# Partial sums of an MLP added to blocks in DRAM by GpSimd's adding DMAs instead of by VectorE in SBUF

## The chip, the core and the metric

The kernel runs on one core of a Trainium2 chip. Its time is the device time of one execution, in microseconds (us). The core has five queues of instructions that run side by side and wait for each other by semaphores: TensorE (PE in the profile; its weight loads are PEld), VectorE (DVE), ScalarE (ACT), GpSimd (POOL) and SyncE (SP), which here only issues DMAs. SBUF is the memory on the chip, PSUM the one that TensorE writes to, DRAM the memory beside it. Each engine takes its instructions strictly in the order in which they stand in its queue, so an instruction that waits holds up all behind it.

## The reference

```python
xn = layernorm(x)                                    # x: 2048 x 576, float32
a  = xn @ dft_hid_re.T ;  b = xn @ dft_hid_im.T      # 576 x 576 each
y  = dft_seq_re @ a - dft_seq_im @ b                 # 2048 x 2048 each
m  = relu(xn @ w1) @ w2                              # w1: 576 x 4608, w2: 4608 x 576
out = x + y + m
```

The result is the sum of x, a two-dimensional Fourier transform (its real part) and an MLP, all of the same normalized x.

## The kernel before

All products are made with fp16 operands split into a high and a low part, three matmuls for one product, summed in float32 in PSUM.

**Stages.** First x is loaded, normalized, split and transposed, in 16 tiles of 128 rows, four of which make a group (`NG` = 4 groups of 512 rows); the first steps of the MLP are woven in between, and the last four tiles (12 to 15) are normalized while the first products of the second layer run. Then comes the MLP (`NB` = 9 blocks of 512 hidden columns, each for the 4 groups: 36 steps), then the transform along the hidden dimension (`dft1`), then the one along the sequence.

**A step of the MLP** computes the hidden columns of one block for one group (`mlp1_step`, L291 and L316, then relu and split in `mlp1_out`, L331 to L342), while the second layer (`mlp2`, L356) of the step before runs between: four parts of `mlp1` and, after them, products 0 and 1, 2 and 3, 4 and 5, and 6. These seven products are those of a fast (Strassen-like) scheme: the group's 512 x 576 result is cut into four blocks (row, column), and `PRODUCTS` says which block each product adds to. In the list below the last two figures are that block's row and column; where the third entry is `False`, the product accumulates onto an earlier one in PSUM (`PLACE`), whose running sum is then added to another block, too.

```python
PRODUCTS = [(A11, B11, True, 0, 0), (A12, B21, True, 0, 0), (S2, T2, False, 0, 1),
            (S1, T1, True, 1, 1), (S3, T3, False, 1, 1), (S4, B22, False, 0, 1), (A22, T4, False, 1, 0)]
PLACE = [0, 1, 0, 3, 0, 3, 0]
```

After each product VectorE adds the PSUM sum, times a scale `us[b]`, to a block of the float32 accumulator `accs[g]` in SBUF (L362). The accumulator starts as x itself, since x is loaded into it (`load_x`), and the normalization reads it there. There are two PSUM buffers for products (`ps2`); the transposes of x use the same two. A product that goes into a buffer, or accumulates onto it, waits until its last sum has been read.

When the last block's product 6 of a group is added, the group's four tiles are stored to DRAM (`spill`, L365), and the memory of `accs` is given to the transforms, whose first results `R` lie there. In the last stage `load_out` loads the stored sums again, and L851 adds the transform to them.

**Beside this**, `prepare_block` readies the weights of the next block in small steps: maxima (L98, then over partitions by GpSimd, L104), scales (L107 to L112, L422 to L432), splits (L165 on ScalarE, L166 on VectorE), sums of w2's blocks (L438 to L441). `passes` loads the matrices of the sequence transform once to sum their magnitudes on ScalarE (L663). The order of instructions on each engine is worked out by a scheduler when the program is built; `tc.issue_after(order["acc"])` puts an instruction of VectorE behind the newest addition to the accumulator.

Of the kernel before, what the change touches and what calls it, by code (L numbers as in the profile page):

```python
# [1 line left out]

# [7 lines left out]
F32 = mybir.dt.float32  # L10
BF16 = mybir.dt.bfloat16
I32 = mybir.dt.int32
AF = mybir.ActivationFunctionType
ALU = mybir.AluOpType
# [3 lines left out]
P = 128  # L18
S = 2048
D = 576  # L20
DFF = 4608
NT = S // P
FB = 512
NB = DFF // FB
# [3 lines left out]
NG = S // G  # L28
TG = G // P
# [4 lines left out]
EH = D // 2  # L34
# [7 lines left out]
def kernel(  # L42
# [17 lines left out]
    nc = tc.nc  # L60
# [3 lines left out]
    dram = ctx.enter_context(tc.tile_pool(name="dram", bufs=1, space=bass.MemoryType.DRAM))  # L64
# [8 lines left out]

    accs = [accp.tile([P, TG, D], F32, name=f"acc{g}") for g in range(NG)]
    acc = [accs[t // TG][:, t % TG] for t in range(NT)]
    spill = [dram.tile([P, D], F32, name=f"spill{t}") for t in range(NT)]
    raws = {}

    def load_x(t):
# [16 lines left out]
    def magnitude(dst, src):  # L96

        nc.vector.tensor_reduce(dst, src, AX.XY, ALU.max, apply_absolute_value=True)  # L98

    def power(s, p, m):  # L100

        n = m.shape[-1]
        top = small.tile([P, 16], F32, tag="top", name="top")[:, :n]
        nc.gpsimd.partition_all_reduce(top, m, P, ReduceOp.max)  # L104
        yield
        half = small.tile([P, 16], F32, tag="half", name="half")[:, :n]
        nc.vector.tensor_scalar(half, top, 2.0**-100, 0.5, ALU.max, ALU.mult)  # L107
        nc.vector.tensor_scalar(  # L108
            s.bitcast(I32), half.bitcast(I32), EXPONENT, EXPONENT,
            ALU.bitwise_and, ALU.bitwise_xor,  # L110
        )
        nc.vector.tensor_scalar(  # L112
            p.bitcast(I32), half.bitcast(I32), EXPONENT, None, ALU.bitwise_and
        )
# [45 lines left out]
    def cell(tag, n=NQ):  # L160
        return small.tile([P, n], F32, tag=f"c_{tag}", name=f"c_{tag}", bufs=2)
# [9 lines left out]
    means, factors, shifts, order = {}, {}, {}, {}  # L171
# [115 lines left out]
    w1s, w2s, us, hs = {}, {}, {}, {}  # L287

    def mlp1_group(b, g, i, cols, ps, wk=WK, start=True, stop=True):
        for n, (kx, hl, k) in enumerate(wk):  # L290
            nc.tensor.matmul(  # L291
                ps[:, cols], w1s[b, i // 2][:, hl, i % 2 * KT + k], xT[g][:, kx, cols],
                start=(start and n == 0), stop=(stop and n == len(wk) - 1),
            )

    def new_ps1(b, g, i):
        return ps1.tile([P, G], F32, tag="ps1", name=f"p1_{b}_{g}_{i}")

    def mlp1(b, g, i):
        ps = new_ps1(b, g, i)  # L300
        mlp1_group(b, g, i, slice(0, G), ps)
        return ps
# [39 lines left out]
        order["lo"] = nc.vector.tensor_tensor(lo, st[:, 1:], hi, ALU.subtract).ins  # L342

    places = {}

    def mlp2(b, g, n):

        qa, qb, first, row, col = PRODUCTS[n]
        if first:
            places[n] = ps2.tile([P, 2, 512], F32, tag="ps2", name=f"p2_{b}_{g}_{n}")[:, :, :EH]  # L350
        ps = places[PLACE[n]]
        for c in range(2):
            for i in range(NQ):
                h, w = hs[b, g, i], w2s[b, i]
                for j, (x, y) in enumerate(((0, 0), (0, 1), (1, 0))):
                    nc.tensor.matmul(  # L356
                        ps[:, c], h[:, x, qa, c * P : (c + 1) * P], w[:, y, qb],
                        start=first and i == 0 and j == 0, stop=i == NQ - 1 and j == 2,
                        skip_group_check=not first,
                    )  # L360
        o = accs[g].rearrange("p (h c) (j e) -> p h j c e", h=2, j=2)[:, row, col]
        order["acc"] = nc.vector.scalar_tensor_tensor(o, ps, us[b], o, ALU.mult, ALU.add).ins  # L362
        if b == NB - 1 and n == 6:
            for t in range(g * TG, (g + 1) * TG):
                nc.sync.dma_start(spill[t], acc[t])  # L365

    sc, pw, mx = {}, {}, {}

    def max_w1(b, f):

        i, r = divmod(f, 2)
        if f == 0:
            mx["w1", b], sc["w1", b], pw["w1", b] = cell("mw1"), cell("sw1"), cell("pw1")
        if r == 0:
            mx["f", b] = cell("mf", 2)
            mx["b", i] = small.tile([P, 1], BF16, tag=f"mb{i}", name=f"mb{b}_{i}") if b < 2 else None
        with tc.issue_after(order["acc" if b > 1 else "lo"]) if b else nullcontext():
            magnitude(mx["f", b][:, r : r + 1], raws["w1", b, i][:, r * KT : (r + 1) * KT])
        if r:
            m = mx["w1", b][:, i : i + 1] if b > 1 else mx["b", i]  # L380
            nc.vector.tensor_reduce(m, mx["f", b], AX.X, ALU.max)

    def later(step):

        with tc.issue_after(order["acc"]):
            next(step, None)

    def power_w1(b, i):
# [62 lines left out]
    def prepare_w1(b, i):  # L451
        p = power_w1(b, i)
        return [
            lambda: max_w1(b, 2 * i),
            lambda: (max_w1(b, 2 * i + 1), b > 1 and next(p)),
            lambda: later(p),
        ], [
            lambda: split_w1(b, 2 * i),
            lambda: split_w1(b, 2 * i + 1),
        ]  # L460
# [40 lines left out]
    ps = [ps1.tile([P, G], F32, tag="ps1", name=f"p1_0_0_{i}") for i in range(NF)]  # L501
# [15 lines left out]
    fill(64)  # L517

    weave(stats([0]), no, no, no, lambda: max_w1(0, 0))
    N(0)  # L520
    max_w1(0, 1)
# [66 lines left out]
    T(10)  # L588
    T(11)
    early = [mlp1(0, 2, 0), mlp1(0, 2, 1)]  # L590
    for q in range(7):
        mlp2(0, 0, q)

# [15 lines left out]
    def power_d(j):  # L609
        if j == 0:  # L610
            sc["d"], pw["d"], mx["d"] = cell("sd", 4), cell("pd", 4), cell("md", 4)
        m = slice(j, j + 1)
        with tc.issue_after(order["acc"]):
            magnitude(mx["d"][:, m], raws["d", j])
        yield from power(sc["d"][:, m], pw["d"][:, m], mx["d"][:, m])

# [24 lines left out]
    NP = NT // 2  # L641
# [28 lines left out]
    for n in range(2, len(steps)):  # L670
        b, g = steps[n]
        pb, pg = steps[n - 1]
        if g == 0 and b:
            if b + 1 < NB:
                todo += prepare_block(b + 1)
            else:
                todo += [lambda: (load_d(0), load_d(1)), lambda: None, new_d, lambda: None]
                for j in range(4):
                    d = power_d(j)
                    todo += [lambda d=d: next(d), lambda d=d, j=j: (later(d), split_d(j))]  # L680
                    if j < 2:
                        todo += [lambda j=j: load_d(j + 2), lambda: None]
                todo += [scales_d]
# [3 lines left out]
        ps = []  # L687
        for i in range(NF):
# [6 lines left out]
            if b == 0 and g + 1 < NG:  # L695
                t = (g + 1) * TG + i
# [15 lines left out]
    for q in range(7):  # L712
        mlp2(*steps[-1], q)
# [109 lines left out]
    def load_out(p):  # L823
        o = outs[p] = op.tile([P, 2, D], F32, tag="o", name=f"o{p}")
        for h in range(2):
            nc.sync.dma_start(o[:, h], spill[p + h * NP])

    AHEAD = 3
    load_out(0)
    for n, (p, kh) in enumerate(units):  # L830
        if kh == 0 and p + 1 < NP:
            load_out(p + 1)
        if n + 1 < len(units):
            load_c(n + 1)
        for i, (q, rq, first, row, col) in enumerate(PRODUCTS):
            m = n * 7 + i
            if m + AHEAD < 7 * len(units):
                operand(m + AHEAD)
            if first:
                places[i] = bank(f"p{n}_{i}")  # L840
            ps, w = places[PLACE[i]], csp[m]
            for k in range(HK):
                r = R[kh * HK + k]
                for j, (a, c) in enumerate(((0, 0), (0, 1), (1, 0))):
                    nc.tensor.matmul(  # L845
                        ps, w[:, a, k], r[:, c, rq],
                        start=first and k == 0 and j == 0, stop=k == HK - 1 and j == 2,
                        skip_group_check=not first,
                    )
            o = outs[p][:, row, col * EH : (col + 1) * EH]  # L850
            nc.vector.scalar_tensor_tensor(o, ps, us["c"][:, n : n + 1], o, ALU.mult, ALU.add)  # L851
            if kh and i in (2, 4, 5, 6):
                h, j = ((0, 0), (1, 1), (0, 1), (1, 0))[(2, 4, 5, 6).index(i)]
                rows = slice((p + h * NP) * P, (p + h * NP + 1) * P)
                e = slice(j * EH, (j + 1) * EH)
                nc.sync.dma_start(out[rows, e], outs[p][:, h, e])
# [54 lines left out]
```

## Time and profile before

| | us |
|---|---|
| median of 3 runs | 1286.96 (1286.81 to 1287.19) |
| profiled execution, its own time | 1287.1 |
| its span in the trace | 1285.3 |
| first addition to the accumulator (L362) | starts at 68.91 |
| one step of the MLP, in the steady part | 22.16 |
| last matmuls of `mlp2`, first stores of the last group | about 842 |

The span runs from the first to the last instruction of the trace; 1.8 us of the execution's time lie around it. In the lines of the profile, a group of instructions reads: line, engine, operation, what is written <- what is read, shape, count | busy us in total, mean ns of one | idle time of the engine ahead of them, and who ended it. In a timeline the first two figures are the start and the length in us.

### The profile page before, as it was taken

What the parts mean: (1) busy time and instruction counts of PE and PEld (TensorE: products, weight loads), DVE (VectorE), ACT (ScalarE), POOL (GpSimd) and SP (SyncE); (2) the same over time, 40 slices, a digit from 0 to 9 for tenths busy, and PEclk for the clock granted to TensorE, in tenths of its full rate; (3) what the DMA queues carried; (4) which work ended last, traced back from release to release, by engine and by line L of the source; (5) the groups of instructions that cost most, each with busy time, mean ns of one, the idle gap of its engine ahead of it and who ended that gap; (6) DMA issues with size and microseconds to landing.
All of it is one profiled execution on the core that took longest, in us unless ns stands there. A gap on an engine that the chain in (4) does not pass through costs nothing.

```text
span 1285.3 us, 21854 instructions
## 1 busy us (share of the span) xinstructions
PE 1267.4 (99%) x9164; PEld 862.8 (67%) x9164; DVE 982.2 (76%) x1671; ACT 539.0 (42%) x794; POOL 34.1 (3%) x60
## 2 busy tenths in 40 slices
PE   8799999999999999999999999999999999999998
PEld 7565666666565665666565665677777777777777
DVE  8978877786686687777867878567678787888875
ACT  4834343443443443534434434234443334333332
POOL 2210000000000000000000000000000000000000
PEclk9999999999999999999999999999999999999999
DMA  6002112221222222222222313330023435344320
GB/s 242 35 8 61 56 65 91 86 73 69 87 91 67 65 79 68 68 91 87 70 70 87 96 58 109 122 120 18 1 106 126 157 101 168 112 133 132 130 85 19
DMA packets 38002, 112.75 MB, mean 88 GB/s; under 512 B 3984, under 2 KB 10640, under 8 KB 37904
## 3 DMA queue, kind: packets, MB, share of 16 engines
q1 hardware_dynamic: 37904, 111.36, 25.9%
q8 instruction: 71, 1.16, 0.4%
q14 instruction: 27, 0.22, 0.1%
HBM read 101.91 MB, written 9.44 MB: 87 GB/s over the span
## 4 chain that ended last, share of the span: by engine, by line
PE 91%; DVE 4%; DMA 2%; ACT 2%; issue 1%; SPq 0%; POOLq 0%; ACTq 0%; DVEq 0%
PE p L291 29%; PE p L356 27%; PE p L845 26%; PE pd L743 7%; PE p L316 1%; DMA raw_w<-in_w_dram 1%; DVE acc L362 1%; DMA acc<-in_x_dram 0%; ACT xT L248 0%; DMA f<-in_cre_dram 0%; DMA c<-in_cre_dram 0%; DVE xn L225 0%; DVE w1s L166 0%; DVE w2s L166 0%; ACT xn L226 0%
## 5 line engine op out<-in xcount | busy, mean ns | idle before, releaser
L291 PE MATMUL p<-xT,w1s 128*128 128x512 f16 (+1 forms) x2136 | 435.4, 355 | 1.5 <-ACT xT L248 1.1
L356 PE MATMUL p<-w2s,h 128*128 128x288 f16 x3024 | 394.4, 286 | 0.4 <-DVE h L342 0.2
L356 PEld LDWEIGHTS <-h 128*128 128x128 f16 x3024 | 295.3, 98 | 101.1 <-issue 0.9
L845 PE MATMUL p<-R,cs 128*128 128x288 f16 x2688 | 329.4, 286 | 0.0
L291 PEld LDWEIGHTS <-w1s 128*128 128x128 f16 x2136 | 192.7, 98 | 201.3 <-issue 18.0
L845 PEld LDWEIGHTS <-cs 128*128 128x128 f16 x2688 | 263.0, 98 | 66.3
L362 DVE SCALAR_TENSOR_TENSOR acc<-p,c_ub,acc 128x576 f32<-128x576 f32 x252 | 204.6, 813 | 38.4 <-PE p L356 38.0
L165 ACT ACTIVATE cs<-c,sc_c 128x1024 f16<-128x1024 f32 x112 | 128.5, 1149 | 200.5 <-PE p L845 147.3
L166 DVE SCALAR_TENSOR_TENSOR cs<-c,sc_c,cs 128x1024 f16<-128x1024 f32 x112 | 143.6, 1283 | 50.3 <-ACT cs L165 50.2
L335 DVE SCALAR_TENSOR_TENSOR h<-p,h 128x256 f16<-128x256 f32 (+1 forms) x144 | 79.7, 555 | 94.3 <-ACT h L334 94.1
L341 ACT ACTIVATE h<-s 128x1024 f16<-128x1024 f32 x72 | 76.1, 1057 | 161.3 <-DVE s L339 161.3
L334 ACT ACTIVATE h<-p 128x512 f16<-128x512 f32 (+1 forms) x144 | 69.8, 486 | 143.9 <-PE p L291 141.6
L342 DVE TENSOR_TENSOR h<-s,h 128x1024 f16<-128x1024 f32 x72 | 88.1, 1224 | 31.4 <-ACT h L341 30.4
L743 PE MATMUL pd<-dsp,xT 128*128 128x288 f16 x896 | 110.4, 286 | 0.1
L743 PEld LDWEIGHTS <-xT 128*128 128x128 f16 x896 | 87.7, 98 | 22.5 <-issue 0.5
L851 DVE SCALAR_TENSOR_TENSOR o<-p,us_c,o 128x288 f32<-128x288 f32 x112 | 57.5, 513 | 20.0 <-PE p L845 19.9
L663 ACT ACTIVATE f<-f 128x1024 f32<-128x1024 f32 x64 | 66.7, 1041 | 3.7 <-DMA f<-in_cre_dram 3.7
L331 ACT ACTIVATE s<-p 128x256 f32<-128x256 f32 x72 | 27.5, 381 | 71.8 <-PE p L316 54.4
L165 ACT ACTIVATE w2s<-raw_w,c_sw 128x576 f16<-128x576 f32 (+1 forms) x54 | 43.9, 850 | 26.1 <-DVE raw_w L439 15.6
L166 DVE SCALAR_TENSOR_TENSOR w2s<-raw_w,c_sw,w2s 128x576 f16<-128x576 f32 (+1 forms) x54 | 48.3, 914 | 7.6 <-ACT w2s L165 7.6
L166 DVE SCALAR_TENSOR_TENSOR w1s<-raw_w,c_sw,w1s 128x640 f16<-128x640 f32 x36 | 30.8, 894 | 9.9 <-ACT w1s L165 9.9
L165 ACT ACTIVATE w1s<-raw_w,c_sw 128x640 f16<-128x640 f32 x36 | 27.9, 819 | 23.8 <-DVE c_sw L108 23.6
(102 smaller groups left out, 663.2 us busy)
## 6 DMA issues: line engine op xcount, KB each, us to landing
f<-in_cre_dram SPq DMA_DIRECT2D x32, 512.0 KB, 3.5
f<-in_cim_dram SPq DMA_DIRECT2D x32, 512.0 KB, 3.5
c<-in_cre_dram SPq DMA_DIRECT2D x32, 512.0 KB, 4.3
c<-in_cim_dram SPq DMA_DIRECT2D x32, 512.0 KB, 4.5
raw_w<-in_w_dram SPq DMA_DIRECT2D x17, 640.0 KB, 4.0
raw_w<-in_w_dram SPq DMA_DIRECT2D x18, 576.0 KB, 3.7
acc<-in_x_dram SPq DMA_DIRECT2D x16, 288.0 KB, 6.0
spill<-acc SPq DMA_DIRECT2D x16, 288.0 KB, 2.5
```

Of the source, the lines that this page charges most:

```text
L165: nc.scalar.activation(hi, src, AF.Copy, scale=s)
L166: nc.vector.scalar_tensor_tensor(lo, src, s, hi, ALU.mult, ALU.subtract)
L291: nc.tensor.matmul(ps[:, cols], w1s[b, i // 2][:, hl, i % 2 * KT + k], xT[g][:, kx, cols], start=(start and n == 0), stop=(stop and n == l ...
L334: nc.scalar.activation(hi, src, AF.Relu)
L335: stt(lo, src, 0.0, hi, ALU.max, ALU.subtract)
L341: order["s"] = nc.scalar.activation(hi, st[:, 1:], AF.Copy).ins
L342: order["lo"] = nc.vector.tensor_tensor(lo, st[:, 1:], hi, ALU.subtract).ins
L356: nc.tensor.matmul(ps[:, c], h[:, x, qa, c * P : (c + 1) * P], w[:, y, qb], start=first and i == 0 and j == 0, stop=i == NQ - 1 and j == 2 ...
L362: order["acc"] = nc.vector.scalar_tensor_tensor(o, ps, us[b], o, ALU.mult, ALU.add).ins
L663: nc.scalar.activation(f, f, AF.Abs, scale=2.0**-10, accum_out=sums_c[:, n, q : q + 1])
L743: nc.tensor.matmul(ps[j], xT[g][:, kx, c * P : (c + 1) * P], dsp[j][:, hl, k], start=(n == 0), stop=(n == len(XK) - 1),)
L845: nc.tensor.matmul(ps, w[:, a, k], r[:, c, rq], start=first and k == 0 and j == 0, stop=k == HK - 1 and j == 2, skip_group_check=not first,)
```

## The change

The sum of a product is no longer added by VectorE to the accumulator in SBUF. ScalarE copies it from PSUM, times the scale, into one of four slots of `accs[0]` in turn, and GpSimd issues a DMA that adds the slot to the block in DRAM. There is one DRAM tile for each block (group, row, column), laid out so that a partition holds its two rows of 288 floats next to each other; SyncE copies x into these tiles beforehand, from DRAM to DRAM (16 DMAs), and the output loads read them in 32 halves instead of 16 whole tiles. The stores of the sums at the end of the MLP go. Where steps were put behind the newest addition of VectorE, they are put behind the newest split in `mlp1_out`.

```diff
-    spill = [dram.tile([P, D], F32, name=f"spill{t}") for t in range(NT)]
+    spill = {
+        (g, row, col): dram.tile([P, TG // 2, EH], F32, name=f"spill{g}_{row}{col}")
+        for g in range(NG) for row in range(2) for col in range(2)
+    }
...
+    turns = itertools.count()
+
+    def spill_x(g):
+        for row in range(2):
+            for col in range(2):
+                src = x[(g * TG + row * 2) * P : (g * TG + row * 2 + 2) * P, col * EH : (col + 1) * EH]
+                nc.sync.dma_start(spill[g, row, col], src.rearrange("(c p) e -> p c e", p=P))
 
     def mlp2(b, g, n):
...
-        o = accs[g].rearrange("p (h c) (j e) -> p h j c e", h=2, j=2)[:, row, col]
-        order["acc"] = nc.vector.scalar_tensor_tensor(o, ps, us[b], o, ALU.mult, ALU.add).ins
-        if b == NB - 1 and n == 6:
-            for t in range(g * TG, (g + 1) * TG):
-                nc.sync.dma_start(spill[t], acc[t])
+        o = accs[0][:, next(turns) % TG].rearrange("p (c e) -> p c e", e=EH)
+        nc.scalar.activation(o, ps, AF.Copy, scale=us[b])
+        nc.gpsimd.dma_start(spill[g, row, col], o, accum_op=ALU.add)
...
-        with tc.issue_after(order["acc" if b > 1 else "lo"]) if b else nullcontext():
+        with tc.issue_after(order["lo"]) if b else nullcontext():
             magnitude(mx["f", b][:, r : r + 1], raws["w1", b, i][:, r * KT : (r + 1) * KT])
...
     def later(step):
-        with tc.issue_after(order["acc"]):
+        with tc.issue_after(order["lo"]):
             next(step, None)
...
     early = [mlp1(0, 2, 0), mlp1(0, 2, 1)]
+    for g in range(NG):
+        spill_x(g)
     for q in range(7):
         mlp2(0, 0, q)
...
     def load_out(p):
         o = outs[p] = op.tile([P, 2, D], F32, tag="o", name=f"o{p}")
         for h in range(2):
-            nc.sync.dma_start(o[:, h], spill[p + h * NP])
+            g, c = divmod(p + h * NP, TG)
+            for col in range(2):
+                nc.sync.dma_start(o[:, h, col * EH : (col + 1) * EH], spill[g, c // 2, col][:, c % 2])
```

More of the change, by code (lines that the diff above doesn't have):

```diff
@@ L1 @@
+import itertools
 from contextlib import ExitStack, nullcontext
@@ L612, in power_d @@
         m = slice(j, j + 1)
-        with tc.issue_after(order["acc"]):
+        with tc.issue_after(order["lo"]):
             magnitude(mx["d"][:, m], raws["d", j])
```

## The prediction

> **What bounds the kernel now.** I read the page's busy times first, then the busy time by stage, then who TensorE waited for, then the timeline where the changed step begins and in one steady stretch, and the instructions' order in the built programs.
>
> ```profile
> span 1285.3 us, 21854 instructions
> ...
> PE 1267.4 (99%) x9164; PEld 862.8 (67%) x9164; DVE 982.2 (76%) x1671; ACT 539.0 (42%) x794; POOL 34.1 (3%) x60
> ```
>
> ```profile
> 50.00:100.00 50.00, 45.66 (x327) 29.05 (x325) 42.42 (x87) 27.71 (x45) 6.01 (x8) 0.97 0.08 27
> 100.00:200.00 100.00, 99.13 (x624) 58.61 (x623) 82.67 (x163) 43.20 (x71) 1.11 (x3) 1.00 0.21 70
> ...
> 400.00:500.00 100.00, 100.00 (x634) 60.29 (x632) 75.58 (x141) 41.73 (x70) 1.43 (x4) 1.00 0.23 73
> ```
>
> In the second fence the columns after a stretch and its length are busy us of TensorE, its weight loads, VectorE, ScalarE and GpSimd, then the granted clock, the DMA share and GB/s. TensorE is never idle between 400 and 500 us, at full clock; VectorE, at 75.58 of 100, is the next busiest and not the bound. The idle time that other engines could give back near the change is 4.34 us between 50 and 100 and 0.87 us between 100 and 200. The change takes no matmul away, so TensorE's 1267.4 us stay.
>
> ```profile
> PE pt L241 <- DVE acc L362: 0.6, 1, 0.6
> ```
>
> This is the only wait worth naming that TensorE has on the step that goes (total us, times, longest us): 0.6 us, once.
>
> **What goes and what comes.**
>
> ```profile
> L362 DVE SCALAR_TENSOR_TENSOR acc<-p,c_ub,acc 128x576 f32<-128x576 f32 x252 | 204.6, 813 | 38.4 <-PE p L356 38.0
> ```
>
> ```profile
> L165 ACT ACTIVATE w2s<-raw_w,c_sw 128x576 f16<-128x576 f32 x36 | 26.6, 771 | 23.7 <-DVE raw_w L439 15.6 <-DVE raw_w L441 8.1
> ```
>
> VectorE loses 252 additions of 813 ns, 204.6 us, all beside TensorE's work. ScalarE gets 252 scalings of 576 columns; the nearest row, of the same width and with a scale from memory, says 771 ns, so 194 us. A step of the MLP takes 22.16 us (timeline below), with seven products: per 100 us ScalarE goes from 41.7 to 66 and VectorE from 75.6 to 50. As loads, both are covered by TensorE's 100, so the sum for them is 0; what they cost as queues is below.
>
> GpSimd gets 252 adding DMAs of 288 KB. No row shows one, so its landing time L (from issue) is bounded:
>
> ```profile
> f<-in_cre_dram SPq DMA_DIRECT2D x32, 512.0 KB, 3.5
> ...
> acc<-in_x_dram SPq DMA_DIRECT2D x16, 288.0 KB, 6.0
> spill<-acc SPq DMA_DIRECT2D x16, 288.0 KB, 2.5
> o<-spill SPq DMA_DIRECT2D x16, 288.0 KB, 3.3
> ```
>
> A plain write of as much to DRAM lands in 2.5 us; that is the lower end. A read and then a write would be 3.3 + 2.5 = 5.8 us, the upper end (6.0 us, in the crowd of the first loads, says the same). Between: 224 KB more cost 1.0 us (3.5 against 2.5), so a second read of 288 KB costs about 1.3 us and an add 3.8 us; some 0.7 us for GpSimd's own issue, which no row shows, makes 4.5 us, my value. The Trainium skill ("DMA: Bandwidth & Descriptors", section on the anatomy of one DMA on the SWDGE path) gives 2.0 us + bytes/436e3 per us for a DMA issued by GpSimd; an estimate from it for 294,912 bytes is 2.7 us, and the lag below would then be some 2.1 us, within what can be told from no change.
>
> Where does L bite? Three things now wait for a landing. The second add to a block waits, on GpSimd, for the first one's landing (products 0 and 1, 3 and 4, 2 and 5 of a group share blocks). The scaling of product n waits, on ScalarE, for the add of product n-4, as there are four staging slots. And whatever stands behind either in its queue waits too: on GpSimd the fp16 remainders of the last four x tiles and the maxima over partitions, on ScalarE the relus and the copies of transposes.
>
> *First use, 69 to 90 us.* All seven products of group 0 come in one burst, and group 1's follow.
>
> ```profile
> 68.58 9.15 PE L356 MATMUL p<-w2s,h 128*128 128x288 f16 x73
> 68.91 0.82 DVE L362 SCALAR_TENSOR_TENSOR acc<-p,c_ub,acc 128x576 f32<-128x576 f32 x1 [0.32 <-PE p L356]
> ...
> 74.26 1.06 DVE L225 TENSOR_SCALAR xn<-acc,mv,r 128x576 f32<-128x576 f32 x2
> ...
> 75.37 0.31 POOL L230 TENSOR_TENSOR xn<-xn 128x64 f16<-128x64 f32 x1 [25.86 <-DVE xn L225]
> 75.64 1.16 POOL L233 TENSOR_TENSOR xn<-xn 128x512 f16<-128x512 f32 x1
> ...
> 78.38 0.66 PE L241 MATMUL pt<-ident,xn 128*128 128x128 f16 x9 [0.65 <-DVE acc L362]
> ...
> 84.64 0.67 PE L241 MATMUL pt<-ident,xn 128*128 128x128 f16 x9
> ```
>
> With L = 4.5, 0.77 us a scaling, and 0.5 us of GpSimd's queue per issue (an allowance, no row): product 0 is scaled by 69.7, add 0 lands at 74.2; add 1 goes then, add 2 at 74.7. In the new order of GpSimd's queue tile 12's remainder stands here, 0.31 + 1.16 = 1.5 us: 75.2 to 76.7. Then add 3, landing at 81.2; then the remainders of tiles 13 to 15, from 77.2 to about 81.8; only then add 4, which also needs add 3's landing (81.2), so it goes at 81.8 and lands at 86.3. Group 1's product 1 is the one that uses add 4's slot: it is scaled by 87.1, and the transposes of tile 13 need its PSUM buffer, as one of two is held by product 0. They start at 87.1 where they started at 84.64: 2.5 us later. In the new TensorE order two matmuls of 512 columns (0.22 us each) and seven of 288 (0.12 us each), 1.3 us, that stood ahead of them are still to come. Lag: 3.8 us. TensorE is full from then on, so it stays. With L = 2.5 the same chain gives 1.9 us (the remainders alone hold add 4 to 82.0), with L = 5.8 it gives 7.1 us.
>
> A rule that speaks against this place: the Trainium skill ("SBUF — State Buffer", section on the two separate sides) says that descriptors of GpSimd's DMAs can't be written while VectorE runs an operation in a two-port mode. The normalizations at 74 us, 0.53 us for 576 columns where the addition takes 0.81, look like such; add 1 would go up to 0.5 us later, and the lag would be about 4.3 us.
>
> *Steady state.*
>
> ```profile
> 400.70 2.97 PE L291 MATMUL p<-xT,w1s 128*128 128x512 f16 x13
> ...
> 413.53 3.10 PE L356 MATMUL p<-w2s,h 128*128 128x288 f16 x24
> ...
> 419.92 3.10 PE L356 MATMUL p<-w2s,h 128*128 128x288 f16 x24
> ...
> 422.86 2.97 PE L291 MATMUL p<-xT,w1s 128*128 128x512 f16 x13
> ```
>
> The first and last row are the same place one step apart, 22.16 us; 24 matmuls take 422.86 - 419.92 = 2.94 us, a product 1.47. Product 3 is done at 422.86 and scaled by 423.6; add 4 waits for add 3, so it lands at 423.6 + 2L. The next step's product 1 needs that slot; it is done at 413.53 + 2.94 + 22.16 = 438.6, and product 3 needs its PSUM buffer at 419.92 + 1.47 + 22.16 = 443.55. So nothing waits below L = 7.5, and TensorE stands only above L = (443.55 - 0.77 - 423.6)/2 = 9.6 us. The term is 0. If that cover goes, each us of L above 9.6 costs 2 us per step.
>
> *The rest.* SyncE gets 16 copies of x to DRAM ahead of the weight loads:
>
> ```profile
> 24.51 0.33 SPq L84 DMA_DIRECT2D raw_w<-in_w_dram  x1
> 59.88 1.39 SPq L90 DMA_DIRECT2D raw_w<-in_w_dram  x2
> ```
>
> By the order, all but the first copy stand behind the load that was issued at 24.51 us; at 6.0 to 8.5 us each (a read in a crowd, and a write), eight in flight, two rounds end by 42 us: hidden before this load and the first add; if they took over 35 us, the load would start late. At the end of the MLP, stores of the sums leave SyncE (0); by the order, ScalarE's first store into R waits until the last adds have read their slots, since R lies over them.
>
> ```profile
> 853.15 0.50 ACT L761 ACTIVATE R<-pd,c_rho 128x288 f16<-128x288 f32 x1 [1.39 <-DVE T L755]
> ```
>
> By the same chain the last adds land at about 851.4 with L = 4.5, 1.7 us before this; with 5.8 at 854.0, 0.9 us after it. The output loads, twice as many and half as large, are a whole unit ahead: 0.
>
> Sum: 3.8 us, with ends 1.9 and 7.1 + 0.9 = 8.0. The profiled execution itself took 1287.1 us (span 1285.3), 0.1 above the median of 1286.96; 1286.96 + 3.8 gives **1290.7**, own range 1288.9 to 1295.0. About 0.2%, 2.57 us, is what can be told from no change here.
>
> **The rivals.**
> *Covered after all (not slower).* The chain turns on add 4's landing: below L of about 3.2 us the lag is under 2.57 us. For it: a plain write lands in 2.5 us. Against: an add must read what it adds to, and the remainders alone give 1.9. Time 1288.9.
> *Faster.* It would take half of the 5.2 us that TensorE idles between 50 and 200 us, of which the change frees 0.6; or a better order by chance: 1284.
> *ScalarE late in the steps that split w2.*
>
> ```profile
> 456.96 0.78 ACT L165 ACTIVATE w2s<-raw_w,c_sw 128x576 f16<-128x576 f32 x1 [0.59 <-DVE raw_w L441]
> ...
> 457.84 3.10 PE L356 MATMUL p<-w2s,h 128*128 128x288 f16 x24
> ```
>
> In the new order product 6's scaling stands behind the first row, so it ends at 457.74 + 0.77 = 458.5, while the second product of the second row needs its buffer at 459.3: 0.8 us to spare. VectorE, on which that split waits, is rid of three additions there (2.4 us), which speaks against it. If four more scalings push ScalarE 2.8 us behind, each of eight blocks costs 2 us: +16 + 3.8, 1306.8; with 2.7 us each, 1312.
> *Adds over 9.6 us*, as small pieces or a slow adder: at 11 us, 2 x 1.4 us x 35 steps = 98 us, 1385. Against: the upper bound of 5.8.
> *The change doing something else*: the order shows 252 adds and no addition on VectorE; no chance given.
>
> **Chances.** Forecast 0.49, covered 0.22, ScalarE 0.14, slow adds 0.12, faster 0.03. Slower by over 0.2%: 0.49 + 0.14 + 0.12 = 0.75; within: 0.22; faster: 0.03. The range 1287.0 to 1312.0 leaves out the slow adds and the faster case, 0.15, and a little at the edges.
>
> **What would show it.** Right: adds that land in 4 to 5 us; a wait of TensorE's transposes of 2 to 4 us between 78 and 90 us, ended by ScalarE; 100.00 of 100 from 200 to 800; ScalarE near 66, VectorE near 50. Wrong: TensorE waits for ScalarE once per block (the split) or in every step (landing over 9.6 us), or copies of x that hold the loads after 60 us.

## The result, and the profile after

The changed kernel takes 1351.47 us (median of 4 runs, 1345.56 to 1358.60), the kernel before 1286.88: a ratio of 1.0503, 95% interval 1.0480 to 1.0527, 64.6 us slower. Forecast were 1290.7 us, with a range to 1312.0. The profiled execution of the changed kernel took 1358.6 us; its rows stand against that time.

From its page, the span, the busy times, GpSimd's DMA queue and some of the DMA issues (how many, KB each, median us from issue to landing):

```profile
span 1356.7 us, 22568 instructions
PE 1281.7 (94%) x9164; PEld 865.4 (64%) x9164; DVE 803.6 (59%) x1419; ACT 698.0 (51%) x1046; POOL 252.4 (19%) x312
...
q0 software_dynamic: 36288, 74.33, 35.7%
...
spill<-acc POOLq DMA_DIRECT2D x252, 288.0 KB, 7.7
f<-in_cre_dram SPq DMA_DIRECT2D x32, 512.0 KB, 6.0
f<-in_cim_dram SPq DMA_DIRECT2D x32, 512.0 KB, 7.6
```

The adds land in 7.7 us, where 4.5 were taken and 5.8 was the upper end. The loads `f`, which share the DMA engines, went from 3.5 to 6.0 and 7.6 us. TensorE's share fell from 99% to 94%.

Busy time by stage, in the columns of the prediction's table (GpSimd's is the last before the clock, the DMA share and GB/s):

```profile
50.00:100.00 50.00, 39.50 (x275) 25.31 (x273) 28.51 (x64) 30.97 (x51) 15.72 (x20) 0.97 0.46 82
100.00:200.00 100.00, 89.94 (x560) 52.08 (x560) 51.83 (x109) 56.73 (x91) 22.63 (x27) 0.98 0.69 132
...
400.00:500.00 100.00, 95.17 (x587) 55.95 (x586) 50.12 (x101) 58.70 (x97) 27.46 (x33) 0.98 0.82 162
...
800.00:900.00 100.00, 91.09 (x581) 55.82 (x580) 45.23 (x84) 53.23 (x84) 29.54 (x37) 0.99 0.83 157
```

TensorE is short by 6.2 us between 50 and 100 (39.50 against 45.66), by 9.2 between 100 and 200, and by 2.6 to 5.5 in each 100 us from 200 to 800 (24.6 us in the six stretches together). VectorE is near 50, as forecast; neither it nor ScalarE is near full. The DMA engines went from 0.23 to 0.82.

Who waited for whom (total us, times, longest us):

```profile
POOL spill L376 <- DMA spill<-acc: 303.5, 43, 10.2
...
ACT acc L375 <- DMA spill<-acc: 185.9, 93, 6.6
...
POOL spill L376 <- ACT f L676: 124.8, 14, 9.7
...
DVE half L112 <- POOL top L109: 56.8, 25, 9.7
...
PE p L368 <- ACT acc L375: 40.5, 31, 2.8
```

The chain starts in the first line: an add stands in GpSimd's queue until an earlier add to the same block has landed. From there it goes on by two ways. Either ScalarE's next scaling stands until its slot is free (second line). Or the maxima over partitions stand behind the adds in the same queue, VectorE waits for them to make the scale of the next weights (fourth line), and ScalarE's split of those weights waits for the scale, with a scaling behind it. Both end in the last line: TensorE's next product stands until ScalarE has emptied its PSUM buffer.

Both ways count. From 200 to 800 us TensorE waits 24.3 us in 21 waits, each for a scaling. Going back on ScalarE from each, the last thing that it had stood for was a free slot in 10 of them (9.7 us) and the scale of weights in 11 (14.6 us); in each of those 11 the maximum stood right behind adds that had waited. One of the 11:

```profile
438.40 0.15 DVE L112 TENSOR_SCALAR half<-top 128x1 f32<-128x1 f32 x1 [1.95 <-POOL top L109]
...
439.00 0.83 ACT L170 ACTIVATE w1s<-raw_w,c_sw 128x640 f16<-128x640 f32 x1 [3.13 <-DVE c_sw L113]
439.74 0.72 ACT L375 ACTIVATE acc<-p,c_ub 128x576 f32<-128x576 f32 x1
...
440.51 1.63 PE L368 MATMUL p<-w2s,h 128*128 128x288 f16 x12 [1.73 <-ACT acc L375]
```

The steady round around it on GpSimd, from its timeline:

```profile
422.56 2.64 POOL L376 DMA_DIRECT2D spill<-acc  x3 [6.87 <-DMA spill<-acc]
425.37 0.86 POOL L376 DMA_DIRECT2D spill<-acc  x1 [0.16 <-issue]
435.39 2.64 POOL L376 DMA_DIRECT2D spill<-acc  x3 [9.16 <-ACT f L676]
437.05 1.32 POOL L109 PARTITION_ALL_REDUCE top<-c_mw  x1
445.23 2.66 POOL L376 DMA_DIRECT2D spill<-acc  x3 [6.86 <-DMA spill<-acc]
```

The first row is the adds of products 4, 5 and 6, the second product 0 of the next step, the third products 1, 2 and 3, the last 4, 5 and 6 again. Two landings belong in between. The trace gives the least, the median and the greatest landing time of the adds issued in a short stretch; these are the first add of the burst at 422.56, product 0's at 425.37 (fourth in its burst), and the last two of the burst at 435.39. The longer line is about these two: their records start at 435.9 and 436.5, and the later one, which landed in 8.2 us, is product 3's.

```profile
DMA to landing us min/median/max: 4.2/4.2/4.2
...
DMA to landing us min/median/max: 9.5/9.5/9.5
...
L376 POOL DMA_DIRECT2D spill<-acc x2: 1216/1390/1564, 435.9 to 436.5; - x2
...
DMA to landing us min/median/max: 7.3/7.8/8.2
```

Product 1's add needs product 0's landing: 425.37 + 9.5 = 434.9, and the burst goes at 435.39, although the row names another releaser. Product 4's needs product 3's: 436.5 + 8.2 = 444.7, and it goes at 445.23. Both times half a us lies between the landing and the issue. So the round is two landings, the issues before and between them and these halves, 445.23 - 422.56 = 22.67 us, where a step of the kernel before takes 22.16. In the bursts between 420 and 470 us the first add landed in 4.2 to 6.4 us, the later ones in 6.2 to 9.8 (up to 0.7 us of it behind the issue ahead, as the records of a burst overlap), and each of the two waits is for a last one. While GpSimd waits, scaled products gather, and all go at once when the wait ends: the wait makes the burst, and the burst makes the next wait long. Not every round is explained in full: in the next one product 0's add lands at 457.6, but GpSimd goes on only at 460.02, and nothing in the trace says what held it for these 2.4 us.

### The profile page after: what moved, and what is told of

Its sections match the earlier page's. It is cut to its first block, busy times and chain, and to the rows that moved or that the text cites. A ratio compares the mean times of both kernels' runs of the same rounds, so it can differ in the third digit from the quotient of the medians.

```text
span 1356.7 us, 22568 instructions
## 1 busy us (share of the span) xinstructions
PE 1281.7 (94%) x9164; PEld 865.4 (64%) x9164; DVE 803.6 (59%) x1419; ACT 698.0 (51%) x1046; POOL 252.4 (19%) x312
## 3 DMA queue, kind: packets, MB, share of 16 engines
q0 software_dynamic: 36288, 74.33, 35.7%
## 4 chain that ended last, share of the span: by engine, by line
PE 35%; DMA 35%; issue 7%; DVE 7%; POOL 6%; ACT 4%; SPq 0%; POOLq 0%; ACTq 0%
DMA spill<-acc 34%; PE p L860 23%; PE pd L756 7%; POOL spill L376 5%; PE p L296 2%; PE p L368 2%; ACT acc L375 1%; DVE w2s L171 1%; DVE h L340 1%; ACT f L676 1%; DMA raw_w<-in_w_dram 1%; DMA c<-in_cre_dram 1%; ACT w2s L170 1%; POOL top L109 1%; ACT h L346 0%
## 5 line engine op out<-in xcount | busy, mean ns | idle before, releaser
L368 PE MATMUL p<-w2s,h 128*128 128x288 f16 x3024 | 402.0, 288 | 40.9 <-ACT acc L375 40.5
L376 POOL DMA_DIRECT2D spill<-acc x252 | 223.2, 1134 | 614.5 <-DMA spill<-acc 303.5
L375 ACT ACTIVATE acc<-p,c_ub 128x576 f32<-128x576 f32 x252 | 184.2, 735 | 210.7 <-DMA spill<-acc 185.9
L756 PE MATMUL pd<-dsp,xT 128*128 128x288 f16 x896 | 113.2, 290 | 5.5 <-DVE R L775 5.5
L676 ACT ACTIVATE f<-f 128x1024 f32<-128x1024 f32 x64 | 66.9, 1046 | 20.5 <-DMA f<-in_cim_dram 19.7
```

The costliest lines, as they stand in the source:

```text
L368: nc.tensor.matmul(ps[:, c], h[:, x, qa, c * P : (c + 1) * P], w[:, y, qb], start=first and i == 0 and j == 0, stop=i == NQ - 1 and j == 2 ...
L375: nc.scalar.activation(o, ps, AF.Copy, scale=us[b])
L376: nc.gpsimd.dma_start(spill[g, row, col], o, accum_op=ALU.add)
L676: nc.scalar.activation(f, f, AF.Abs, scale=2.0**-10, accum_out=sums_c[:, n, q : q + 1])
L756: nc.tensor.matmul(ps[j], xT[g][:, kx, c * P : (c + 1) * P], dsp[j][:, hl, k], start=(n == 0), stop=(n == len(XK) - 1),)
```

## The experiments

Theory A, after the result: the adds, not ScalarE's scalings, cost the time, by landings in turn in GpSimd's queue. Rivals: ScalarE's queue; the slots; the DMA engines' load as such.

**e1, plain writes.**

```diff
-nc.gpsimd.dma_start(spill[g, row, col], o, accum_op=ALU.add)
+nc.gpsimd.dma_start(spill[g, row, col], o)
```

> The 252 DMAs from GpSimd write their slot to the block instead of adding to it, so the output lacks the sums; the order, the queue, the slots and the waits on earlier landings stay. If the adding itself is dear (reading the block, adding, writing), a plain write lands in about 2.5 to 4.5 us, the GpSimd queue no longer stands on landings, and the time falls to 1287-1296. If it is the issue from GpSimd and the dependence of one write on the landing of the one before, whatever it does, landing stays near 7 us and the time at 1340-1355.

1293.35 us, ratio 1.0052 (1.0037 to 1.0067). A write landed in 2.4 us, its issue took GpSimd 0.54 us where that of an add took 0.89 (busy time over 252 issues: 136.8 and 223.2 us), and TensorE was at 100.00 of 100 from 200 to 800 us. With the same queue and waits, it is the adding that is dear. GpSimd's DMA queue (packets, MB, share of 16 engines' span):

```profile
q0 software_dynamic: 20160, 74.33, 15.1%
```

Against 36288 packets and 35.7% for the same bytes: 0.357 x 16 x 1356.7 / 252 = 30.8 us of DMA engine time per add, and 0.151 x 16 x 1291.5 / 252 = 12.4 us per write; an add costs 2.5 times as much.

**e2, no adds.** The line above is left out.

> The 252 DMAs are left out, and with them all sums; ScalarE's scalings into the four slots, the copies of x and the output's loads stay. If the loss comes from the adds (landing waits or the load on the DMA engines), the time is 1286-1291. If ScalarE's queue with 252 more instructions behind relus and splits costs something by itself (my rival of ScalarE late in the steps that split w2), 1300-1312; the early part (0 to 100 us) then shows also what the copies of x cost: 1-2 us if TensorE's busy time to 50 us stays at 39.2 where it was 40.9.

1288.29 us, ratio 1.0011 (1.0002 to 1.0021). Busy times by stage:

```profile
100.00:200.00 100.00, 98.63 (x626) 58.86 (x626) 62.41 (x134) 63.56 (x102) 1.10 (x3) 1.00 0.23 77
...
400.00:500.00 100.00, 100.00 (x630) 59.95 (x629) 53.28 (x109) 63.11 (x103) 1.42 (x4) 1.00 0.25 79
```

252 scalings in ScalarE's queue and the 16 copies of x cost 1.3 us together. ScalarE as the late engine falls. The copies cannot be told from nothing in the first 50 us: TensorE's busy time there was 39.63 here with them and 39.85 in e11 without.

**e3, twelve slots.**

```diff
-o = accs[0][:, next(turns) % TG].rearrange("p (c e) -> p c e", e=EH)
+o = acc[next(turns) % 12].rearrange("p (c e) -> p c e", e=EH)
```

> Twelve staging slots in place of four; all else as in the changed kernel. If the loss is ScalarE's wait for a free slot (185.9 us in 93 waits) by a landing time over the cover of four slots, the time falls to 1290-1305. If GpSimd's queue is full by itself (two landings of 7.7 us in turn and five more issues of 1.13 us are 21 of a step's 22.16 us, and the maxima over partitions stand behind them), more slots only lengthen the queue, and the time stays at 1330-1355, with the scales of the weights as the late part.

1322.23 us, ratio 1.0293 (1.0234 to 1.0351): between the two. The profiled execution was the slowest of the four, 1335.74 us. In it ScalarE's wait for slots fell from 185.9 to 8.2 us, TensorE's wait for ScalarE fell from 40.5 to 18.3 us, but GpSimd's wait for landings stayed:

```profile
POOL spill L376 <- DMA spill<-acc: 320.2, 45, 9.7
```

Twelve slots give back 29.2 of the 64.6 us; TensorE's mean over the six stretches from 200 to 800 is 97.85 of 100 (95.90 in the changed kernel). The way by the slots is closed, the way by the weight scales is not: all 12.9 us that TensorE still waits for ScalarE from 200 to 800 us (8 waits) come behind a scale whose maximum stood behind adds, and VectorE waits 54.7 us for maxima there, where it was 35.4 with four slots.

**e4, two sets of blocks**, and **e5, both.**

```diff
+dst = (other if n in (1, 4, 5) else spill)[g, row, col]
-nc.gpsimd.dma_start(spill[g, row, col], o, accum_op=ALU.add)
+nc.gpsimd.dma_start(dst, o, accum_op=ALU.add)
```

> The second product of each block (products 1, 4 and 5) is added to blocks of a second set in DRAM, which is not read at the end, so the output lacks these products; no add waits for the landing of the one before. Four slots, the same number and size of adds. If the two landings in turn per step are the cause, GpSimd's queue falls to 8 us a step and the time to 1290-1305, all of the rest early. If the load on the DMA engines is the cause (share 0.8, adds and loads that slow each other), landing stays over 7 us, the wait for slots stays, and the time at 1325-1350.

> Both relaxations: products 1, 4 and 5 of each step are added to a second set of blocks that is not read at the end (the output lacks them), and there are twelve slots. Two sets alone gave 1300.04 us, 13 above the kernel before, with TensorE at 100.00 of 100 from 200 to 800 us, 42.98 of 50 between 50 and 100 and 95.00 between 800 and 900. If what is left there is the wait for slots, 1288-1293. If it is the number of bytes that the adds move in a burst (GpSimd's queue and the DMA engines in the first steps, and the last adds at the end), 1297-1302.

1300.04 us (ratio 1.0102, 1.0087 to 1.0117) and 1299.03 (1.0091, 1.0076 to 1.0106). With no add behind another's landing, and all 252 of them, landing falls to medians of 5.3 and 5.2 us and the steady loss is gone, at a DMA share of 0.9, higher than in the changed kernel. So the load on the DMA engines alone does not make the loss. Twelve slots add nothing then. What is left, some 12 us, sits before 200 and after 800 us.

**e6, sums in the slot first.**

```diff
+SLOT = [0, 0, 1, 2, 2, 1, 3]
+o = accs[0][:, SLOT[n]].rearrange("p (c e) -> p c e", e=EH)
+if n in (0, 2, 3, 6):
     nc.scalar.activation(o, ps, AF.Copy, scale=us[b])
+else:
+    nc.vector.scalar_tensor_tensor(o, ps, us[b], o, ALU.mult, ALU.add)
+if n in (1, 4, 5, 6):
     nc.gpsimd.dma_start(spill[g, row, col], o, accum_op=ALU.add)
```

> Products that go to one block are summed in the slot first: ScalarE scales the first one into it, VectorE scales and adds the second, and one DMA adds the sum, so a step has four adds to four different blocks in place of seven with two landings in turn. The output is complete. If landings in turn and the crowd of adds are the cause, landing falls to 4-5.5 us, TensorE stands at 100.00 of 100 in the steady part, and the time is 1288-1296. If any adding DMA behind ScalarE's queue costs (issue of 1.13 us on GpSimd, slots held through a landing), 1300-1320.

1296.07 us, ratio 1.0075 (1.0060 to 1.0090), 0.07 above the first range, complete output; landing 4.4 us, TensorE at 100.00 in the steady part.

**e7, one add per step.**

```diff
+if n == 6:
     nc.gpsimd.dma_start(spill[g, row, col], o, accum_op=ALU.add)
```

> Only product 6 of each step is added (36 adds; the other scalings stay, their adds are left out, and the output lacks them). This measures the landing of an add by itself. If the adding makes a DMA slow, landing stays near 7.7 us with one in flight; if the 7.7 us come from several adds in flight together, it is near the least of the changed kernel, 4.0-4.5 us, and GpSimd's issue near 0.85 us. The time is 1287-1290 either way.

The landing of its adds from 400 to 800 us (least, median, greatest):

```profile
DMA to landing us min/median/max: 4.2/4.2/4.7
```

So an add alone takes 4.2 us, close to the 4.5 of the prediction. The time is 1291.62 us, ratio 1.0031 (1.0019 to 1.0044), higher than expected; e14 looks for the reason.

**e8, without the loads f.**

```diff
-nc.sync.dma_start(f, blocks_c(n)[q])
+if m == 0:
+    nc.sync.dma_start(f, blocks_c(n)[q])     # later m use this f
```

> The 63 loads f of 512 KB that run beside the adds are left out (one is kept and used again, so the scale of the last product is not that of the reference); the adds are as in the changed kernel. If the adds are slow because they share the DMA engines and DRAM with these loads, landing falls to 5 us or less and the time to 1290-1315. If the adds slow each other, landing stays at 7-7.7 us and the time at 1335-1350; ScalarE loses its waits for f (19.7 us) and GpSimd's queue those behind them.

1310.42 us, ratio 1.0173 (1.0154 to 1.0193). The add's median landing is 5.4 us, and from 200 to 800 TensorE is at 100.00 again, with the dependent adds still there: the later adds of a burst at 447.73 landed in 6.7 to 7.2 us, where those of the burst at 445.23 of the changed kernel took 8.3 to 9.8. So the steady loss needs the loads `f`, too. Whether it is by the DMA engines that they share with the adds, or by ScalarE's own waits for `f` (19.7 us in the changed kernel), which go with them, this run does not tell. The early part is as bad as before (39.77 of 50 between 50 and 100 us).

**e9, one wait in turn in place of two** (e4 with products 1 and 5 in the second set).

> Products 1 and 5 go to a second set of blocks that is not read at the end (the output lacks them); only product 4 still waits for the landing of the add before it, product 3's. If the loss is a full GpSimd queue, two landings in turn and seven issues (2 x 7.7 + 7 x 1.13 = 23.3 us in a step of 22.16), one landing less leaves it at about 15 us, TensorE stands at 100.00 of 100 from 200 to 800 us, and the time is 1299-1306, near the 1300.04 of no landing in turn at all. If any wait for a landing in that queue bunches the adds and holds slots too long, about half the steady loss stays: 1315-1330.

1306.51 us, ratio 1.0142 (1.0124 to 1.0159), 100.00 of 100 from 200 to 800, landing 5.8: as the full queue says, though 0.5 us above its range. (The 1.13 us per issue in the expectation is the mean length of overlapping records; with 0.89 its sum is 21.6 us, and only the waited-for landings of 9.5 and 8.2 fill the step.) It is 6.5 us above e4, all of it outside the steady part.

**e10, half of each add.**

```diff
-nc.gpsimd.dma_start(spill[g, row, col], o, accum_op=ALU.add)
+nc.gpsimd.dma_start(spill[g, row, col][:64], o[:64], accum_op=ALU.add)
```

> Each add moves 64 of its 128 partitions (the other half of each product's sum is missing in the output); same number of adds, same waits, same four slots. If the adds' work on the DMA engines is what makes several in flight slow each other (4.2 us for the first of a burst, up to 9.8 for the third), a burst of half the size lands in 3.5-6 us and the time falls to 1293-1305. If landing in turn costs a fixed time per DMA, whatever its size, landing stays at 6.5-7.7 and the time at 1335-1350.

1298.76 us, ratio 1.0080 (1.0062 to 1.0097); landing 3.4 us, no steady loss. The slow landings go with the bytes that the adds move, not with a fixed time per DMA.

**e11, the first block on VectorE.**

```diff
+if b == 0:        # o: the group's accumulator, as in the kernel before
+    nc.vector.scalar_tensor_tensor(o[:, row, col], ps, us[b], o[:, row, col], ALU.mult, ALU.add)
...               # at n == 6: o's four blocks are stored to spill
+    return
-    spill_x(g)
```

> In the first block of the hidden dimension the sums are added by VectorE to SBUF as in the kernel before, then stored; the adding DMAs start with the second block, and the copies of x fall away. All complete. It shows what the first use costs: the changed kernel loses 15 us of TensorE's time between 50 and 200 us. If that loss comes from the burst of adds beside the remainders and from the first steps' queue, it goes, and the time is 1335-1341. If a step that GpSimd's queue can't hold is paid anyway, the first steps too, only four steps' share goes (4-5 us): 1345-1348.

1338.41 us, ratio 1.0395 (1.0375 to 1.0415), 13.1 below the changed kernel. TensorE has 45.66 of 50 between 50 and 100 us, and 98.58 of 100 after. The first use is worth these 13 us, and the steady loss starts just the same without it (94.56 to 97.12 of 100 from 200 to 800).

**e12, a mended version**: e6, with the first block and group 3 on VectorE.

> A version from what the runs showed: the first block and the last group of rows stay on VectorE and SBUF as in the kernel before; elsewhere products of one block are summed in the slot (ScalarE scales, VectorE adds) and one DMA adds the sum, so 96 adds are left, none at the start and none beside the loads at the end of the MLP. The output is complete. If the losses of the version with summed pairs (1296.07) sat only at the start (1.3 us between 100 and 200) and the end (4.5 us between 800 and 900), 1287-1290. If adds in the steady part delay something that is paid at the end (loads of the last stage, scales of the DFT's factors), 1292-1296. Below 1286 is not expected: TensorE bounds both kernels and no matmul is gone.

1293.37 us, ratio 1.0039 (1.0024 to 1.0054), in the second range and not the first. The largest gap is at the end of the MLP, and it starts at the last load `f`: ScalarE stood 5.13 us for its landing, the maximum of the sums on VectorE came after it, and an addition stood behind that, for which TensorE waited 2.26 us. No version with adds beat the kernel before.

**e13 and e15, the dependent adds issued later** (twelve slots; in e15 with `tc.issue_after` on the add before it).

```diff
+adds[n] = spill[g, row, col], o
+for m in {0: (0, 4), 2: (2,), 3: (3, 1), 5: (5,), 6: (6,)}.get(n, ()):
+    if m in adds:
+        nc.gpsimd.dma_start(*adds.pop(m), accum_op=ALU.add)
```

> All 252 adds to the same blocks, complete output, but GpSimd issues the second add of a block later: product 1's add behind product 3's, product 4's behind the next step's product 0, with twelve slots so that they can be held. No byte, load or dependence is gone; only the add that depends on a landing no longer stands directly behind it. If the steady loss is the round that feeds itself (a wait for a landing gathers a burst, and the last of a burst, which the next wait is for, lands in 8-10 us), TensorE stands at 100.00 of 100 from 200 to 800 us and the time is 1297-1303, as with two sets and twelve slots (1299.03). If the bytes with the dependence are enough, whatever the order, it is the 1322 of twelve slots, or 1312-1325.

> The same adds, bytes, loads and dependences with twelve slots as in the kernel before this one, whose order in GpSimd's queue came out as that of twelve slots alone (1322.23 us). Here the order is forced: product 1's add is issued behind product 3's, product 4's behind the next step's product 0. If the loss is the round that feeds itself (the add that depends on a landing stands directly behind the one it depends on and gathers a burst), TensorE is at 100.00 of 100 from 200 to 800 us, landing near 5.2 us as without any add in turn, and the time 1297-1303. If the dependence with these bytes is enough in any order, 1312-1325.

e13 came out with 1325.18 us (1.0295, 1.0276 to 1.0314): the scheduler put the adds back into the order of e3, so it only repeats e3. In e15 the order is the one meant: 1299.06 us, ratio 1.0084 (1.0067 to 1.0101), complete output. Its stage from 400 to 500 us, and what GpSimd's adds waited for:

```profile
400.00:500.00 100.00, 100.00 (x635) 60.55 (x634) 53.27 (x110) 62.00 (x101) 28.55 (x36) 1.00 0.87 164
```

```profile
POOL spill L381 <- ACT acc L376: 507.3, 166, 9.7
...
POOL spill L381 <- DMA spill<-acc: 2.8, 2, 1.9
```

Same adds, bytes, loads and dependences as e3, and 23 us less: GpSimd now waits for ScalarE's products, and for landings 2.8 us in all, where it was 320.2 in e3. So, with twelve slots, the place of the dependent add in the queue makes what is left of the steady loss. With four slots this order was not run, and no run took the maxima out of GpSimd's queue, which might close the same way.

**e14, e7 less its very last add.**

```diff
-if n == 6:
+if n == 6 and (b, g) != (NB - 1, NG - 1):
```

> As the kernel with one add per step (1291.62 us), less the very last one, which ran beside the four loads of the last stage's first factors (35 adds left; the output lacks the rest). If that one add delayed these loads and so TensorE at the start of the DFT (96.04 of 100 between 800 and 900 us, 99.68 without adds), it is 99.3-99.7 there and the time is 1288-1289. If the loss there has another cause (the order of the loads, ScalarE), it stays at 96-97 and 1291-1292.

TensorE by tens of us, first e7, then e14 (busy, clock, DMA share, GB/s):

```profile
840.00:850.00 10.00, 8.04 (x67) 1.00 0.32 100
850.00:860.00 10.00, 8.89 (x72) 1.00 0.51 141
860.00:870.00 10.00, 9.25 (x72) 1.00 0.01 2
```

```profile
840.00:850.00 10.00, 8.08 (x67) 1.00 0.31 107
850.00:860.00 10.00, 10.00 (x84) 1.00 0.28 106
860.00:870.00 10.00, 10.00 (x84) 1.00 0.01 2
```

Half of it is as expected: that add landed in 9.2 us beside the four first loads of the last stage, whose medians were 6.6 and 8.6 us with it and 5.4 without, and it cost TensorE 1.9 us. The other 1.9 us stay: the last load `f` keeps ScalarE waiting 2.19 us, a scaling stands behind it, and TensorE waits 1.92 for that. The medians, 1291.62 and 1290.67 us (1.0023, 1.0014 to 1.0032), are too close to show it by themselves.

## Why the prediction was wrong

**What was right.** The two loads that were costed at nothing cost nothing: VectorE is at 50, ScalarE at 58.7 (63 in e2; a scaling took 735 ns, not 771), and e2 puts all of it at 1.3 us. An add by itself lands in 4.2 to 4.3 us, where 4.5 was taken. The Trainium skill's formula for a DMA issued by GpSimd ("DMA: Bandwidth & Descriptors", anatomy of one DMA), by which 2.7 us is the estimate for this size, comes near the plain write (2.4 in e1) and not the add. The three waits were the right ones, and one sign came true: TensorE's transposes waited 2.36 us for ScalarE at 80.76. That the 4.5 came so near is partly luck: it was added up from loads and stores of other kinds and 0.7 us for GpSimd's issue, a term that no run shows (an issue took 0.88 us of GpSimd's queue, and a lone landing, counted from the start of the issue, 4.2 us in all).

**The step that failed** is "a landing time L" itself: one number for all adds, worked out from rows of single transfers, with 5.8 us as its end. L depends on how many adds are in flight and on the loads beside them: 4.2 us alone, up to 9.8 for the last of a burst. A bound on L from rows of lone DMAs was no bound, and what the adds do to the DMA engines (a share of 0.82 where it was 0.23) was not in the sum at all. A second term was missing: the maxima over partitions were named among what waits behind the adds and then put at nothing without a reason; by them go 14.6 of the 24.3 us that TensorE waits from 200 to 800. The allowance of 0.5 us of GpSimd's queue per issue was low, too: 0.88 in the round above.

**The steady state**, "the term is 0". Its chain was nearly the right one, and its threshold, 9.6 us for TensorE to stand, was for one waited-for landing at the price of any other. In the trace the two landings that are waited for are those that the bursts make slow, 9.5 and 8.2 us, and with the issues and gaps (22.67 - 9.5 - 8.2 = about 5 us) they fill a step. By that round (an estimate from these rows) the queue is full from a landing of (22.16 - 5) / 2 = 8.6 us, and with lone adds it would take 2 x 4.2 + 5 = 13 us. The prediction put adds 4, 5, 6 and 0, and then 1, 2 and 3, nowhere together, so that it had no burst. The steady loss needs both the wait in the queue and slow landings: with all bytes, it goes when both dependent waits of a step go (e4) or one of them (e9) or, with twelve slots, when the dependent add stands later (e15); with the same adds and dependences, it goes when there are fewer bytes (e10) or no loads `f` (e8).

**First use.** The chain was followed rightly and was too short at each link. Add 4 goes at 84.83 (81.8 forecast) and lands in 4.7 us, the transposes follow at 90.39 (87.1 forecast; 84.64 before):

```profile
84.83 3.53 POOL L376 DMA_DIRECT2D spill<-acc  x4 [0.87 <-DMA spill<-acc]
```

```profile
90.39 0.66 PE L246 MATMUL pt<-ident,xn 128*128 128x128 f16 x9 [1.68 <-ACT acc L375]
```

That is 5.75 us late, 2.5 forecast: add 3, for which add 4 waits, left at 78.24 and took 6.3 us behind two others. "TensorE is full from then on" was wrong by more: another 9.2 us go between 100 and 200, in the steps of the first two blocks. There the weights come late. Their load, issued at 99.69 us before, went at 108.05 and took 7.6 us (at most 3.9 before):

```profile
115.67 1.16 ACT L419 ACTIVATE j<-raw_w 128x1152 f32<-128x1152 f32 x1 [7.00 <-DMA raw_w<-in_w_dram]
...
119.04 1.63 PE L368 MATMUL p<-w2s,h 128*128 128x288 f16 x12 [2.63 <-ACT acc L375]
```

Another 2.74 us of TensorE, at 127.69, stand behind the next such load; 2.31 us at 165.77 and 1.28 at 183.62 come by the maxima. VectorE's normalizations, named as a risk for add 1, were over at 74.16, and add 1 went at 75.76, half a us after add 0's landing as elsewhere; so whether they could hold it up is not shown. e11 puts the first block's part of the loss at 13.1 us.

**The rest.** The copies of x are hidden, as costed. The end of the MLP, costed at 0 to 0.9 us, is worth 3.6 us with one add per step (e7, e2: 96.04 against 99.68 of 100 between 800 and 900). By e14, half of that is loads that land late beside the very last add; the other half comes by the last load `f`, whose lateness no run takes apart.

**The rivals.** ScalarE late in the steps that split w2 is refuted by e2. "Adds over 9.6 us" came nearest, in its place and its sign, but with the wrong reason: not small pieces or a slow adder (4.2 us alone), but bursts. The loss does not stand on one mechanism: from the changed kernel, twelve slots give back 29.2 us (e3) and the later issue of the dependent adds another 23.2 (e15), together 52.4 of the 64.6; the last 12 sit before 200 and after 800 us. The waits tell which way TensorE was held (slots or weight scales), but no run took the maxima out of the queue by themselves.

## What to carry to other kernels

A landing time read from lone transfers is a price only while few are in flight; where many DMAs wait on each other in one queue, follow one round in the queue, add up the landings that are waited for with the values of a full queue, and compare the sum with the step. Then ask what else stands in that queue, and who waits for it: here it was the maxima. A DMA that depends on the landing of another should not stand directly behind it: issuing it a few places later, or summing the pair in SBUF first, took away the steady loss here (the first with twelve slots). And TensorE, already full, gained nothing from relief on VectorE: all that the change did to it was make it wait.

## What the runs showed of the hardware

An adding DMA of 288 KB used 36288 / 252 = 144 packets and 30.8 us of DMA engine time, a plain write 80 packets and 12.4 us; one add beside four loads of 512 KB held them up by some 1 to 3 us. GpSimd's time for an issue was 0.54 us for a write and 0.87 to 0.89 for an add, in the crowded kernel, too. The longer means in its rows are records that start while the instruction ahead still runs:

```profile
L376 POOL DMA_DIRECT2D spill<-acc x252 | 223.2, 1134 | 614.5 <-DMA spill<-acc 303.5 <-ACT f L676 124.8 <-ACT acc L375 94.9
L109 POOL PARTITION_ALL_REDUCE top<-c_mw x21 | 20.3, 965 | 8.5 <-issue 7.9 <-DVE c_mw L392 0.6
```

The first row's busy time makes 223.2 / 252 = 0.89 us per issue. A maximum took 360 ns before; in the round above it ends at 437.05 + 1.32 = 438.37, only 0.34 us after the burst ahead of it (435.39 + 2.64 = 438.03), so it is not slower, but later.

Part of the loss is not idle time. The same 9164 matmuls were busy 1281.7 us, 14.3 more than before, and the mean granted clock was 0.990 against 0.997. In these rows the clock falls in or behind stretches in which TensorE stood:

```profile
110.00:120.00 10.00, 7.01 (x46) 1.00 0.34 83
120.00:130.00 10.00, 7.26 (x38) 0.87 0.71 127
920.00:930.00 10.00, 6.39 (x29) 0.66 0.01 2
```

It did not fall in every such stretch: from 160 to 170 us TensorE was busy 7.69 of 10, at a clock of 1.00. No run took this apart from the waits.
